# Loading q of the first token pairs in rows of 16 tokens and sorting it on TensorE, in a fused retention and bilinear feed-forward kernel

## The chip, the cores and the metric

The kernel runs on one core of one Trainium2 chip. The metric is the device time in microseconds; several runs are reported by their median. All durations below come from one profiled execution of the kernel before.

## The reference

A recurrence over time (retention with a decay per head), followed by a bilinear feed-forward layer on the 3072 = 4 x 768 tokens.

```python
# q, k, v: (4 batches, 8 heads, 768 tokens, 64), float32
gamma = 1.0 - 2.0 ** (-5.0 - np.arange(H))
for t in range(S):
    state = gamma * state + einsum('bhd,bhe->bhde', k[:, :, t], v[:, :, t])
    y[:, :, t] = 1 / sqrt(D) * einsum('bhd,bhde->bhe', q[:, :, t], state)
x = y.transpose(0, 2, 1, 3).reshape(3072, 512)
out = (x @ w_a) * (x @ w_b) @ w_out        # w_a, w_b: 512 x 1536, w_out: 1536 x 512
```

## The kernel before

**Attention.** The tokens are cut into 24 slots of 128. A decay per head becomes two tables: k is scaled by exp(-position x log gamma), q by exp(+position x log gamma) / 8, so that within a batch the retention is a masked product of q and k plus a running state. For each slot: the scaled copies `kqb` and `vb` (bf16) are made, k and q are turned so that the head dimension lies on the partitions (`kqT`), the scores `at` are formed on TensorE and masked by VectorE into `aT`, the state `st` is summed in PSUM and copied by ScalarE or VectorE (`gbd`, `gst`), and `y` is the sum of a part from the state (`inter`) and a part from the slot itself (`intra`). It is copied to `xt`, which has the feature on the partitions and is what the feed-forward layer reads.

**Pairs.** Slots 0 to 5 are handled two at a time as pairs 0, 1 and 2. `load_pair` (L93) puts two neighbouring tokens on one partition, so that one contiguous piece in memory has 2 x 64 x 4 = 512 bytes. k and q are turned on TensorE by products with the identity (`flip2`, L341; `tp`, L348), and copied from PSUM by ScalarE and VectorE (L179). `scores2`, `update2`, `inter2`, `intra2` and `leave2` (L351 to L415) are the pairs' versions of the steps. Slots 6 to 9 are turned on TensorE too (`flip`, L231), slots 10 to 23 by transposing transfers (`casts`, L225).

**Feed-forward.** Token tiles of 4, 2, 4, 4, 4, 4 and 2 slots. For tile J and each of 12 blocks `ft` of 128 features, `ffn_a` (L429) makes a = x w_a in PSUM, ScalarE copies it (`asb`, L432), `ffn_g` (L439) makes g = x w_b, and VectorE multiplies the two into `ht` (L441). `ffn_out` (L455) multiplies with w_out, ScalarE copies the result (`osb`, L177) and issues the store from its own queue (L461). Three PSUM buffers, tag `ff`, are shared in turn by a, g, o, the turned tiles and some of the scores.

**Order.** Nothing is left to a scheduler: `seq` chains every instruction of an engine to the one before in the order in which the Python runs, and the last part of the kernel writes that order out by hand. All loads stand in the SyncE queue, in the order of `LOADS`:

```python
LOADS = "p0 p1 w0 w1 w2 w3 w4 p2 w5 o0 o1 o2 o3 o4 o5 s6 s7 s8 s9 s10 s11".split()
```

(p: k, q, v of a pair; w: a sixth of w_a and of w_b; o: a sixth of w_out; s: k, q, v of a slot.) From slot 10 on, the transposing transfer of slot t and then the loads of slot t + 2 are issued from the same queue. The framework gives every transfer one of eight completion semaphores in turn, and a transfer's issue waits until the previous one on the same semaphore has landed. GpSimd (POOL) makes most of the scaled copies and casts all weights to bf16.

The tables are made at the beginning for the pairs (`tables`, L134) and during the third feed-forward block for the other slots (`late_tables`, L165).

Of the kernel before, what the change touches and what calls it, by code (L numbers as in the profile page):

```python
# [24 lines left out]
def kernel(  # L25
# [25 lines left out]
    MID = S // 2  # L51

# [40 lines left out]
    def load_pair(u):  # L93
        for nm, src in (("k", k), ("q", q), ("v", v)):
            f = raw.tile([P, H, 2, D], F32, tag=nm + "f", name=nm + "f")
            s = src[0, :, 2 * u * P : 2 * (u + 1) * P, :].rearrange("h (p two) d -> p h two d", two=2)
            seq(nc.sync.dma_start(out=f, in_=s))
            for par in range(2):
                raws[nm, 2 * u + par] = f[:, :, par, :]
# [24 lines left out]
    issue_loads(6)  # L124
    lgr = const.tile([P, 1, H], F32, name="lgr")
# [8 lines left out]
    def tables(pattern, channel):  # L134
        posp = const.tile([P, NCH, 1], F32, name=f"posp{channel}")
        seq(nc.gpsimd.iota(posp, pattern=pattern, base=-MID, channel_multiplier=channel,
                           allow_small_or_imprecise_dtypes=True))
        earg = const.tile([P, NCH, H], F32, name=f"earg{channel}")
        seq(nc.vector.tensor_tensor(earg, posp.to_broadcast([P, NCH, H]),
                                    lgr.to_broadcast([P, NCH, H]), op=ALU.mult))  # L140
        ktab = const.tile([P, NCH, H, 1], F32, name=f"ktab{channel}")
        qtab = const.tile([P, NCH, H, 1], F32, name=f"qtab{channel}")
        seq(nc.scalar.activation(ktab[:, :, :, 0], earg, AF.Exp, scale=-1.0))
        seq(nc.scalar.activation(qtab[:, :, :, 0], earg, AF.Exp, bias=bq))
        tabs.append((ktab, qtab))

    tables([[2 * P, PAIRS], [1, 2], [0, 1]], 2)
    make_identity(nc, ident)
# [4 lines left out]
    for par in range(2):  # L153
        m = const.tile([P, 1, P], BF16, name=f"mask{par}")
        seq(nc.gpsimd.memset(m, 1.0))
        for c in range(2):
            mc = m[64 * c : 64 * c + 64]
            seq(nc.gpsimd.affine_select(out=mc, in_=mc, compare_op=ALU.is_ge, fill=0.0,
                                        base=-par, pattern=[[0, 1], [1, 2], [2, 64]],
                                        channel_multiplier=-2))  # L160
        masks.append(m)
# [8 lines left out]

    wa_bf = wpool.tile([P, KT, DFF], BF16, name="wa_bf")
# [28 lines left out]
    def scaled(eng, t, i):  # L200
        ktab, qtab = tabs[0] if t < 2 * PAIRS else tabs[1]
        dst, src, tab = kqb[t][:, i], raws["kq"[i], t], (ktab, qtab)[i][:, t % NCH]
        if t < 2 * PAIRS:
            dst, src = (x.rearrange("p (hp r) d -> p hp r d", r=2) if x is src else x
                        for x in (dst, src))
            tab = tab.rearrange("p (hp r) o -> p hp r o", r=2).to_broadcast([P, HP, 2, D])
        else:
            dst = dst.rearrange("p hp r d -> p r hp d")
            src = src.rearrange("p (r hp) d -> p r hp d", r=2)
            tab = tab.rearrange("p (r hp) o -> p r hp o", r=2).to_broadcast([P, 2, HP, D])  # L210
        seq(eng.tensor_tensor(dst, src, tab, op=ALU.mult))  # L211
# [119 lines left out]
    kqT2 = {}  # L331

    def casts2(u, on):
        for t in (2 * u, 2 * u + 1):
            new_nat(t)
        for (i, par), eng in on.items():
            scaled(eng, 2 * u + par, i)
        for t in (2 * u, 2 * u + 1):
            cast(nc.gpsimd, vb[t], raws["v", t])

    def flip2(u, i, on):  # L341
        if i == 0:
            kqT2[u] = tra.tile([P, 2, 2, HP, P], BF16, tag="kqT2", name="kqT2", bufs=2)
        for pars, eng in on:
            tp = psff.tile([P, 2, HP, P], BF16, tag="ff", name="tp")[:, : len(pars)]
            for n, par in enumerate(pars):
                for hp in range(HP):
                    seq(nc.tensor.transpose(tp[:, n, hp, :], kqb[2 * u + par][:, i, hp, :, :], ident))  # L348
            cast(eng, kqT2[u][:, pars[0] : pars[0] + len(pars), i], tp)

    def scores2(u, par, ff=False):  # L351
# [6 lines left out]
        for hp in range(HP):  # L358
            for c in range(2):
                for r in range(2):  # L360
                    seq(nc.tensor.matmul(at[r][half(c), hp, :],  # L361
                                         kqT2[u][half(r), par, 0, hp, half(c)],
                                         kqT2[u][half(r), :, 1, hp, half(c)],
# [6 lines left out]
    def update2(u, c):  # L370
# [5 lines left out]
        for par in range(2):  # L376
            for hp in range(HP):
                for r in range(2):
                    t = 2 * u + par
                    seq(nc.tensor.matmul(st[half(r), hp, :], kb[t][half(c), hp, r, :],  # L380
                                         vb[t][half(c), 2 * hp + r, :],
# [5 lines left out]
    def inter2(u):  # L387
        for c in range(2):
            if (u, c) == (0, 0):
                continue  # L390
            for hp in range(HP):
                seq(nc.tensor.matmul(ys[u][c][:, hp, :], gbd[c][:, hp, :],
                                     kqT2[u][:, :, 1, hp, half(c)], start=False, stop=False,
                                     skip_group_check=True))

    def intra2(u, par, begin):
# [3 lines left out]
        for hp in range(HP):  # L400
            for r in range(2):
                for c in range(2):
                    seq(nc.tensor.matmul(ys[u][c][half(r), hp, :], vb[t][half(c), 2 * hp + r, :],  # L403
                                         aT[t][half(c), r, hp, :],
                                         start=(begin and hp == 0), stop=not begin,
                                         skip_group_check=True))

    def leave2(u):
        J, i = where[2 * u]
        if i == 0:  # L410
            xt[J] = xtp.tile([P, KT, 4 * P], BF16, tag="xt", name="xt")
        for c, eng in enumerate((nc.scalar, nc.vector)):
            cast(eng,
                 xt[J][:, :, (i + c) * P : (i + c + 1) * P].rearrange(
                     "p k (n two) -> p k two n", two=2),  # L415
                 ys[u][c].rearrange("p k (two n) -> p k two n", two=2))
# [5 lines left out]
    def ffn_a(J, ft, c0=0, c1=None):  # L422
# [5 lines left out]
        for kt in range(KT):  # L428
            seq(nc.tensor.matmul(a, wa_bf[:, kt, fs], xt[J][:, kt, c0:c1],  # L429
# [4 lines left out]
    def ffn_g(J, ft, c0=0, c1=None):  # L434
# [3 lines left out]
        for kt in range(KT):  # L438
            seq(nc.tensor.matmul(g, wb_bf[:, kt, fs], xt[J][:, kt, c0:c1],  # L439
# [7 lines left out]
    def ffn_out(J, i):  # L447
# [4 lines left out]
        for c0, c1 in cols:  # L452
# [5 lines left out]
            if c0 == DM // 2:  # L458
                continue
            b0 = DM // 2 if c0 else 0  # L460
            seq((nc.sync if c0 else nc.scalar).dma_start(out=out[n0 : n0 + P, b0:c1],  # L461
                                                         in_=osb[:, b0:c1]))
# [15 lines left out]
    K, Q = 0, 1  # L478
    casts2(0, {(K, 1): D_, (K, 0): D_, (Q, 1): D_, (Q, 0): D_})
    flip2(0, K, [((0, 1), A_)])  # L480
    flip2(0, Q, [((1,), D_), ((0,), D_)])
# [3 lines left out]
    casts2(1, {(K, 0): G_, (K, 1): G_, (Q, 0): G_, (Q, 1): D_})  # L485
    intra2(0, 1, True)
    inter2(0)
    intra2(0, 0, False)
    leave2(0)
    flip2(1, K, [((0, 1), A_)])  # L490
    update2(0, 1)
    flip2(1, Q, [((1,), D_), ((0,), D_)])
    scores2(1, 0)
    scores2(1, 1, True)
# [3 lines left out]
    intra2(1, 0, True)  # L498
    inter2(1)
    ffn_a(0, 0, 0, W2)  # L500
    ffn_a(0, 1, 0, W2)
    intra2(1, 1, False)
    leave2(1)
# [8 lines left out]
    for ft in range(2, NFT):  # L512
        if ft == 3:
            late_tables()
        if ft % FPW == 0 and ft // FPW + 1 < NW - 1:
            cast_w(ft // FPW + 1)
        if ft == 8:
            casts2(2, {(K, 0): G_, (Q, 0): G_})
            cast_w(NW - 1)
        if ft < 10:  # L520
            ffn_ab(0, ft)
        if ft == 8:
            scaled(D_, 5, K)
            scaled(D_, 5, Q)
    flip2(2, K, [((0, 1), A_)])
    flip2(2, Q, [((0, 1), D_)])
    scores2(2, 0)
    update2(2, 0)
    ffn_a(0, 10)
    scores2(2, 1)  # L530
    ffn_a(0, 11)
    intra2(2, 0, True)
    inter2(2)
    ffn_g(0, 10)
    intra2(2, 1, False)
    leave2(2)
# [49 lines left out]
```

## Time and profile before

| what | value |
|---|---|
| median of 3 runs (lowest, highest) | 240.75 us (237.88, 241.6) |
| the profiled execution: time, span | 237.4 us, 235.7 us |
| TensorE busy | 219.6 us, 93% of the span |
| VectorE, ScalarE, GpSimd busy | 96.1, 83.2, 78.6 us |
| TensorE's first instruction | 6.5 us after the span's start |
| first product of feed-forward tile 0, 1, 2 | 18.97, 47.01, 78.83 us |
| HBM read, written | 28.31 MB, 6.29 MB |
| sixth store of the output: copied, issued | 79.62, 81.19 us |

How to read it: the span is the time from the first to the last instruction of the profiled execution; the time of that execution is 1.7 us longer. Busy times say how long an engine worked, not whether anyone waited for it. In lines of the timeline the first number is the start, the second the length, both in us; then engine, line of the kernel, operation, output and inputs, shapes, count; in brackets the idle time before and what ended it. A queue that issues transfers is written SPq or ACTq. In lines of the waits, "A <- B: 7.2, 3, 6.5" says that A waited for B 7.2 us in total, 3 times, at longest 6.5 us. In the chain, each line is a start, a length and the work that stands on the chain.

### The profile page before, as it was taken

To read this page: it belongs to the slowest core of one execution; us is meant where nothing else is said; L and a number is where in the kernel's file an instruction comes from. 1 tells how busy PE (TensorE), PEld (TensorE's weight loads), DVE (VectorE), ACT (ScalarE), POOL (GpSimd) and SP (SyncE) were. 2 spreads that over 40 slices of the span, in tenths; PEclk is the share of its full clock that TensorE was granted. 3 is DMA by queue.
4 is the path that set the end of the run, shared out by engine and by line. 5 is a ranking of instruction groups with operands and counts; after the bars stand their busy time and mean duration, and the time that the engine had idled before them with its cause. 6 is when DMAs were issued, how large, how long until landed. Compare 5 with 4: busy or idle time off the path is not lost.

```text
span 235.7 us, 4955 instructions
## 1 busy us (share of the span) xinstructions
PE 219.6 (93%) x2021; PEld 121.6 (52%) x2044; DVE 96.1 (41%) x170; ACT 83.2 (35%) x162; POOL 78.6 (33%) x99
## 2 busy tenths in 40 slices
PE   0788997999999899999999999999999999999995
PEld 0566444488555344545454544454544444445874
DVE  3766347655254055634045640155630124310530
ACT  2243523443114423524234521344512242312422
POOL 3385766787763454445335530000000000000000
PEclk9999999999999999999999999999999999999999
DMA  6999999999999999999999982200002200012102
GB/s 179 290 333 352 335 273 376 342 198 219 234 260 211 245 252 172 243 181 257 210 255 172 230 93 89 89 4 0 3 0 89 89 3 0 0 47 89 45 3 89
DMA packets 91894, 38.59 MB, mean 164 GB/s; under 512 B 71776, under 2 KB 87392, under 8 KB 91872
## 3 DMA queue, kind: packets, MB, share of 16 engines
q1 hardware_dynamic: 88416, 32.12, 64.4%
q10 hardware_dynamic: 3456, 6.16, 7.3%
q8 instruction: 16, 0.26, 0.5%
q14 instruction: 6, 0.05, 0.1%
HBM read 28.31 MB, written 6.29 MB: 147 GB/s over the span
## 4 chain that ended last, share of the span: by engine, by line
PE 77%; DMA 11%; DVE 5%; issue 2%; SPq 2%; POOL 1%; ACT 1%; ACTq 0%; DVEq 0%; POOLq 0%
PE g L439 24%; PE a L429 24%; PE o L455 20%; DMA kf<-in_k_dram 6%; DMA qf<-in_q_dram 5%; PE at L254 2%; PE y L299 1%; DVE aT L367 1%; POOL kqb L211 1%; SPq L91 1%; PE tp L348 1%; PE st L270 1%; PE y L403 1%; DVE ht L441 1%; DVE kqT L179 1%
## 5 line engine op out<-in xcount | busy, mean ns | idle before, releaser
L441 DVE TENSOR_TENSOR ht<-g,asb 128x512 bf16<-128x512 f32 (+1 forms) x86 | 52.0, 604 | 109.8 <-PE g L439 88.7
L439 PE MATMUL g<-xt,wb_bf 128*128 128x512 bf16 (+1 forms) x340 | 76.0, 344 | 1.7 <-ACT asb L432 0.8
L429 PE MATMUL a<-xt,wa_bf 128*128 128x512 bf16 (+1 forms) x334 | 75.3, 344 | 0.8 <-DVE xt L179 0.2
L432 ACT CAST asb<-a 128x512 bf16<-128x512 f32 (+1 forms) x86 | 44.2, 517 | 69.4 <-PE a L429 63.6
L455 PE MATMUL o<-wo_bf,ht 128*128 128x512 bf16 (+2 forms) x303 | 63.7, 362 | 0.5
L439 PEld LDWEIGHTS <-wb_bf 128*128 128x128 bf16 x344 | 33.4, 98 | 30.3 <-issue 1.3
L429 PEld LDWEIGHTS <-wa_bf 128*128 128x128 bf16 x344 | 32.7, 98 | 27.9 <-DVE xt L179 0.7
L455 PEld LDWEIGHTS <-ht 128*128 128x128 bf16 x312 | 29.2, 98 | 31.5
L177 ACT COPY osb<-o 128x512 f32<-128x512 f32 (+2 forms) x25 | 14.1, 565 | 53.2 <-PE o L455 41.2
L211 POOL TENSOR_TENSOR kqb<-kf,ktab 128x512 bf16<-128x512 f32 x21 | 21.9, 1044 | 26.6 <-DMA kf<-in_k_dram 26.6
L211 POOL TENSOR_TENSOR kqb<-qf,qtab 128x512 bf16<-128x512 f32 x20 | 21.4, 1068 | 3.1 <-DMA qf<-in_q_dram 2.4
L259 DVE TENSOR_TENSOR aT<-at,mask 128x512 bf16<-128x512 f32 x36 | 22.3, 680 | 0.0
L179 POOL CAST vb<-vf 128x512 bf16<-128x512 f32 x24 | 14.5, 612 | 20.6 <-DMA vf<-in_v_dram 10.6
L348 PE MATMUL tp<-ident,kqb 128*128 128x128 bf16 x48 | 5.5, 280 | 7.2 <-DVE kqb L211 7.2
L308 ACT CAST xt<-y 128x512 bf16<-128x512 f32 x18 | 9.7, 589 | 3.2 <-PE y L299 3.2
L367 DVE TENSOR_TENSOR aT<-at,mask 128x512 bf16<-128x512 f32 x12 | 7.5, 684 | 2.4 <-PE at L361 2.4
L348 PEld LDWEIGHTS <-kqb 128*128 128x128 bf16 x48 | 4.0, 125 | 8.3 <-DVE kqb L211 7.8
L179 POOL CAST wa_bf<-wsta 128x1024 bf16<-128x1024 f32 x6 | 6.3, 1044 | 4.0 <-DMA wsta<-in_moe_w_a_dram 4.0
L179 POOL CAST wb_bf<-wstb 128x1024 bf16<-128x1024 f32 x6 | 6.3, 1043 | 2.7 <-DMA wstb<-in_moe_w_b_dram 2.7
L179 POOL CAST wo_bf<-wsto 128x1024 bf16<-128x1024 f32 x6 | 6.3, 1042 | 1.9 <-DMA wsto<-in_moe_w_out_dram 1.9
L177 ACT CAST gst<-st 128x256 bf16<-128x256 f32 x12 | 4.5, 373 | 6.7 <-PE st L270 6.7
L254 PE MATMUL at<-kqT 64*64 64x128 bf16 x288 | 5.8, 219 | 0.0
(47 smaller groups left out, 81.9 us busy)
## 6 DMA issues: line engine op xcount, KB each, us to landing
out_dram<-osb ACTq DMA_DIRECT2D x23, 256.0 KB, 2.1
kf<-in_k_dram SPq DMA_DIRECT2D x18, 256.0 KB, 4.6
qf<-in_q_dram SPq DMA_DIRECT2D x18, 256.0 KB, 5.1
vf<-in_v_dram SPq DMA_DIRECT2D x18, 256.0 KB, 5.4
wsta<-in_moe_w_a_dram SPq DMA_DIRECT2D x6, 512.0 KB, 8.8
wstb<-in_moe_w_b_dram SPq DMA_DIRECT2D x6, 512.0 KB, 9.0
wsto<-in_moe_w_out_dram SPq DMA_DIRECT2D x6, 512.0 KB, 8.9
kf<-in_k_dram SPq DMA_DIRECT2D x3, 512.0 KB, 7.1
```

Source lines behind the costliest of these rows:

```text
L177: seq(nc.scalar.copy(dst, src))
L179: seq(engine.tensor_copy(dst, src))
L211: seq(eng.tensor_tensor(dst, src, tab, op=ALU.mult))
L254: seq(nc.tensor.matmul(at[r][half(c), hp, :], kqT[t][half(r), 0, hp, half(c)], kqT[t][half(r), 1, hp, :], start=True, stop=True, skip_grou ...
L259: seq(nc.vector.tensor_tensor(aT[t][:, r], at[r], mask.to_broadcast([P, HP, P]), op=ALU.mult))
L348: seq(nc.tensor.transpose(tp[:, n, hp, :], kqb[2 * u + par][:, i, hp, :, :], ident))
L367: seq(nc.vector.tensor_tensor(aT[t][:, r], at[r], masks[par].to_broadcast([P, HP, P]), op=ALU.mult))
L429: seq(nc.tensor.matmul(a, wa_bf[:, kt, fs], xt[J][:, kt, c0:c1], start=(kt == 0), stop=(kt == KT - 1)))
L432: seq(nc.scalar.copy(asb, a))
L439: seq(nc.tensor.matmul(g, wb_bf[:, kt, fs], xt[J][:, kt, c0:c1], start=(kt == 0), stop=(kt == KT - 1)))
L441: seq(nc.vector.tensor_tensor(ht[J][:, ft, c0:c1], g, asbs.pop((J, ft, c0)), op=ALU.mult))
L455: seq(nc.tensor.matmul(o, ht[J][:, ft, i * P : (i + 1) * P], wo_bf[:, ft, c0:c1], start=(ft == 0), stop=(ft == NFT - 1)))
```

## The change

- q of pairs 0, 1 and 2 is loaded with one partition for each block of 16 tokens and head: a contiguous piece has 16 x 64 x 4 = 4096 bytes. It is scaled by a table `lanes` with a value for each partition and token of the block, and turned by products with columns of the identity (`pick`, a 0/1 matrix), 16 products of 64 x 64 outputs for each half, from which float32 results are copied to `qT2`. Tokens of a pair then stand in the order (token mod 16, block); the stores of the first six slots put the rows back in their places.
- `scores2`, `inter2` and `intra2` read `qT2` in steps and use the head order of the other slots. `inter2` has twice as many products with 64 columns of weights instead of 128.
- The table of the other slots is made at the beginning.
- `xt` of tiles 0 and 1 is laid out by slots, [slot, feature block, token] instead of [feature block, token].
- `warm(n)` issues n products of a zero matrix with 512 zero columns, whose result nobody reads: 28 in all.
- The order in the pairs' steps is changed: the state's second update earlier in pair 0, feed-forward products between the steps of pairs 1 and 2, pair 2 one block earlier, copies on other engines.

```diff
 def load_pair(u):
     for nm, src in (("k", k), ("q", q), ("v", v)):
+        if nm == "q":
+            f = raws[nm, "pair", u] = raw.tile([P, NJ, D], F32, tag="qf", name="qf")      # NJ = 16
+            s = q[0, :, 2 * u * P : 2 * (u + 1) * P, :].rearrange("h (b j) d -> b h (j d)", j=NJ)
+            seq(nc.sync.dma_start(out=f.rearrange("p j d -> p (j d)"), in_=s))
+            continue
...
+    def lane_table():      # called after tables(...) of the pairs; late_tables() follows the masks
+        row = const.tile([P, PAIRS, NJ], F32, name="row")
+        seq(nc.gpsimd.iota(row, ...))
+        start = const.tile([P, NJ, 1], F32, name="start")
+        seq(nc.gpsimd.iota(start, ...))
+        make_identity(nc, ident)
+        lane = ident.rearrange("p (b h) -> p b h", h=H)
+        own = const.tile([P, 2, 1], F32, name="own")
+        for i, val in enumerate((start, lgr)):
+            one = const.tile([P, NJ, H], F32, name=f"one{i}")
+            seq(nc.vector.tensor_tensor(one, lane, val.to_broadcast([P, NJ, H]), op=ALU.mult))
+            seq(nc.vector.tensor_reduce(out=own[:, i], in_=one.rearrange("p b h -> p (b h)"), ...))
+        seq(nc.vector.tensor_scalar(row, row, own[:, 0], own[:, 1], op0=ALU.add, op1=ALU.mult))
+        tab = const.tile([P, PAIRS, NJ, 1], F32, name="lanes")
+        seq(nc.scalar.activation(tab[:, :, :, 0], row, AF.Exp, bias=bq))
+        for r in range(2):
+            seq(nc.vector.tensor_copy(pick[:, r],
+                                      lane[:, :, HP * r : HP * r + HP].rearrange("p b h -> p h b")))
...
 def flip2(u, i, on):       # i == 1: q
+                tq = psff.tile([P, NJ // 2, HP, NJ], F32, tag="ff", name="tq")
+                j0 = NJ // 2 * pars[0]
+                for j in range(NJ // 2):
+                    for r in range(2):
+                        seq(nc.tensor.matmul(tq[half(r), j], ql[u][:, j0 + j, :], pick[:, r], ...))
+                cast(eng, qT2[u][:, j0 : j0 + NJ // 2], tq)
...
 def inter2(u):
-            for hp in range(HP):
-                seq(nc.tensor.matmul(ys[u][c][:, hp, :], gbd[c][:, hp, :],
-                                     kqT2[u][:, :, 1, hp, half(c)], ...))
+            for r in range(2):
+                for hp in range(HP):
+                    seq(nc.tensor.matmul(ys[u][c][half(hp % 2), 2 * r + hp // 2, :],
+                                         gbd[c][:, hp, half(r)],
+                                         qT2[u][:, :, hp, 8 * c : 8 * c + 8], ...))
...
-def leave2(u):
+def leave2(u, on):
-        xt[J] = xtp.tile([P, KT, 4 * P], BF16, tag="xt", name="xt")
+        xt[J] = xtp.tile([P, 4, KT, P], BF16, tag="xt", name="xt")
...
+    def warm(n, pool, tag):
+        idle = pool.tile([P, HP, P], F32, tag=tag, name="idle")
+        for _ in range(n):
+            seq(nc.tensor.matmul(idle, zero[:, 0, :], zero, start=True, stop=True, ...))
...
 def ffn_out(J, i):
+            if J < 2:
+                dst = dst.rearrange("(b j) d -> j b d", j=NJ)
...
+    warm(11, psat, "y1")
     casts2(0, {(K, 1): D_, (K, 0): D_, (Q, 1): D_, (Q, 0): D_})
     flip2(0, K, [((0, 1), A_)])
-    flip2(0, Q, [((1,), D_), ((0,), D_)])
+    warm(3, psat, "y1")
+    flip2(0, Q, [((1,), D_)])
+    warm(1, psat, "y1")
+    flip2(0, Q, [((0,), A_)])
+    warm(3, psat, "y1")
     scores2(0, 1)
     scores2(0, 0, True)
     update2(0, 0)
-    casts2(1, {(K, 0): G_, (K, 1): G_, (Q, 0): G_, (Q, 1): D_})
+    warm(4, psat, "y1")
+    casts2(1, {(K, 0): G_, (K, 1): G_, (Q, 1): D_, (Q, 0): D_})
     intra2(0, 1, True)
     inter2(0)
+    update2(0, 1)
+    warm(2, psff, "ff")
     intra2(0, 0, False)
-    leave2(0)
+    leave2(0, (A_, A_))
+    warm(2, psff, "ff")
     flip2(1, K, [((0, 1), A_)])
-    update2(0, 1)
     flip2(1, Q, [((1,), D_), ((0,), D_)])
-    scores2(1, 0)
-    scores2(1, 1, True)
+    warm(2, psff, "ff")
+    scores2(1, 0, True)
+    scores2(1, 1)
     update2(1, 0)
     cast_w(0)
     intra2(1, 0, True)
+    ffn_a(0, 0, 0, W2)
     inter2(1)
-    ffn_a(0, 0, 0, W2)
+    intra2(1, 1, False)
     ffn_a(0, 1, 0, W2)
-    intra2(1, 1, False)
-    leave2(1)
+    leave2(1, (A_, D_))
...
-        if ft == 8:
-            casts2(2, {(K, 0): G_, (Q, 0): G_})
+        if ft == 7:
+            casts2(2, {(K, 0): G_, (K, 1): G_})
             cast_w(NW - 1)
-        if ft < 10:
+        if ft < 9:
             ffn_ab(0, ft)
-        if ft == 8:
-            scaled(D_, 5, K)
+        if ft == 7:
+            scaled(D_, 4, Q)
             scaled(D_, 5, Q)
     flip2(2, K, [((0, 1), A_)])
-    flip2(2, Q, [((0, 1), D_)])
-    scores2(2, 0)
+    ffn_a(0, 9)
+    flip2(2, Q, [((0,), D_), ((1,), A_)])
+    ffn_g(0, 9)
+    scores2(2, 0, True)
+    scores2(2, 1)
     update2(2, 0)
     ffn_a(0, 10)
-    scores2(2, 1)
-    ffn_a(0, 11)
     intra2(2, 0, True)
     inter2(2)
+    ffn_a(0, 11)
+    intra2(2, 1, False)
+    leave2(2, (A_, D_))
     ffn_g(0, 10)
-    intra2(2, 1, False)
-    leave2(2)
     ffn_g(0, 11)
```

## The prediction

> **What bounds the kernel now.** I read the page's first two parts, then the waits of TensorE, then the timeline of the first 25 us, of 36 to 48 us and of 76 to 84 us, and last the chain.
>
> ```profile
> PE 219.6 (93%) x2021; PEld 121.6 (52%) x2044; DVE 96.1 (41%) x170; ACT 83.2 (35%) x162; POOL 78.6 (33%) x99
> ...
> PE   0788997999999899999999999999999999999995
> ...
> PEclk9999999999999999999999999999999999999999
> DMA  6999999999999999999999982200002200012102
> ```
>
> TensorE is busy for 219.6 of 235.7 us, so at most 16 us can be taken from its idle time. The row of tenths says where that lies: before its first instruction, in the slices up to 22 us, around 37 to 48 us, and (an 8) around 80 us. The DMA row says that the transfers fill the engines for the first 23 slices (135 us): whatever waits for a late transfer moves only if the whole stream moves.
>
> ```profile
> PE tp L348 <- DVE kqb L211: 7.2, 3, 6.5
> PE at L361 <- DVE kqT L179: 1.8, 3, 0.8
> PE y L403 <- DVE aT L367: 1.0, 3, 0.4
> PE g L439 <- ACT asb L432: 0.8, 2, 0.6
> PE g L439 <- DVE xt L179: 0.7, 1, 0.7
> ```
>
> All but one of TensorE's waits are in the three pairs. The fourth row is 0.6 us at 82.2 us, and it decides my forecast (the chain of 78 to 84 us, start, us, what):
>
> ```profile
> 74.98 6.14 DMA qf<-in_q_dram
> ...
> 81.19 0.34 ACTq L461
> ...
> 81.57 0.59 ACT asb L432
> ...
> 82.21 1.02 PE g L439 x4
> ```
>
> ACT has copied the sixth output tile at 79.62 us, but its store starts only at 81.19: in the built program a transfer waits for the one that last used the same of eight completion semaphores, here slot 13's q, which lands at 74.98 + 6.14 = 81.12. Behind the store stands the cast that frees a PSUM buffer, and behind that TensorE's second g of tile 2. TensorE would have been ready at 81.59 and starts at 82.21. From there to the end it is nearly gapless. So there are two clocks: TensorE's own (first 80 us) and the DMA stream's, and at 82 us the later one counts.
>
> **The change on the DMA clock.** Three q loads of 512 KB go from pieces of 512 B to pieces of 4 KB. In the trace k, q and v of pair 0 land at 5.0, 6.8 and 8.6 us, those of pair 1 at 10.45, 12.3 and 14.1: 1.8 us each; q of pair 2 takes 1.6 (32.4 to 34.0). Weight loads of the same size take 1.5 with pieces of 1 KB (15.55, 17.05), and 1.37 with 2 KB (the six wo casts, 40.54 to 47.37, each waiting for its load). 4 KB has no row. Bounds: no gain at all, or the trend carried on to 1.25, which saves 0.55 + 0.55 + 0.35 = 1.45. I take the nearest row, 1.35: 0.45 + 0.45 + 0.25, about 1.2 us earlier for everything loaded behind.
>
> Against this stands a part that nobody would see in the diff. The new order hands out the eight semaphores differently: in the listing of the changed program the sixth store waits for slot 13's **v**, not its q. v is issued at 77.03 and takes 5.2: it lands at 82.23, 1.1 us after q. So the store starts at 82.23 - 1.2 + 0.07 = 81.1 rather than 81.19, and with the same 1.02 us from there to g, TensorE goes on at about 82.1 rather than 82.21. The third and fourth stores now wait for slot 11's v (69.95 - 1.2) and slot 12's k (72.97 - 1.2), so ACT stands for 1 to 2 us each time; behind them are a gst and the xt of slots 6 and 7, which TensorE needs at 75.3, when they are done at about 73.4.
>
> **The change on TensorE's clock, first pairs.** Setup: the lane table adds to DVE one memset, two products, two reductions, a two-scalar operation, two copies and the late earg, and to POOL two iotas beside the moved mask (3 operations). The nearest rows are 0.2 us (earg 0.21, mask memset 0.21, select 0.3). DVE comes to about 4.6 us, POOL, which earg waits for, to 4.2; DVE's first kqb waits for k until 5.15. Cover of 0.5 us, cost nothing; if POOL is 1 us later than I count, 0.5 us. ACT has nothing before 7 us.
>
> q's DVE products start at 6.45 instead of 6.95 (k's products end there). The warm-up products (28 in all, 128x512) occupy TensorE where it stood. Do they help? The granted-clock row is 9 throughout, but equal work is slower early:
>
> ```profile
> 6.50 1.04 PE L348 MATMUL tp<-ident,kqb 128*128 128x128 bf16 x8 [6.50 <-DVE kqb L211]
> ...
> 9.42 1.07 PE L361 MATMUL at<-kqT 64*64 64x128 bf16 x32 [0.51 <-DVE kqT L179]
> ...
> 16.37 0.64 PE L361 MATMUL at<-kqT 64*64 64x128 bf16 x32 [0.51 <-DVE kqT L179]
> ...
> 38.03 0.83 PE L348 MATMUL tp<-ident,kqb 128*128 128x128 bf16 x12
> ```
>
> 130 ns a transpose against 69. A warm-up costs 0.215 us at the fast rate (four FFN products take 0.86), some 0.41 at the slow one, so eleven of them last to 5.0 or 5.7 us, before k is ready. I take the fast rate from 6.5 on; bounds: all fast, or all slow as far as 16 us. The Trainium skill (TensorE: Matmul & The Clock Gate, Part 1) says the clock opens after about 3.4 us of sustained activity; by it the transposes would be fast at 6.5, by the row alone not before about 10 us of sparse work.
>
> The sorting products have 64 columns of weights. The row of that shape is line 270's:
>
> ```profile
> 64.57 0.32 PE L270 MATMUL st<-vb,kqb 128*64 128x64 bf16 x8
> ```
>
> 40 ns each, 0.64 us for a half of 16, where four transposes took 0.28. (The skill's same page, under Fast Weight Load, says that only weights of 128 columns load fast; it would make a 64-column load 53 ns and a half 0.85 us. The row decides.) The PSUM result is f32, so its copy takes ACT's 0.59 or DVE's 0.7 instead of 0.42.
>
> Chain: transposes 6.5 to 7.05; three warm-ups to 7.7; half 1 to 8.35; one warm-up; half 0 to 9.2; ACT's copy 9.3 to 9.9; scores at 9.95 instead of 9.42, 16 of them in 0.42 instead of 0.67; DVE's first aT at 10.45 instead of 10.18: **0.27 later**. The four masked copies take 2.6 us as before. The second half's intra, the xt copies (now both on ACT, 0.6 each, to 15.1) and the k copy behind them (to 16.15, was 15.37) follow, then 32 sorting products (1.28, hidden under that) and DVE's two copies of 0.7 to 16.9; scores at 16.95 instead of 16.37: 0.6 later. Then it gains: the FFN products stand between the steps, and xt by slots lets g read slots 0 and 1 while 2 and 3 are written, where it now waits 0.65 for xt (fifth row of the waits). I reach the first product on slots 2 and 3 at 22.25, now 22.0: **0.25 later**. Bounds: 1.0 earlier (sorting at 27 ns, as the 64x64 products at 40.78, and copies not queued), 3.9 later (slow clock, below).
>
> **Pair 2.** From 37 to 48 us TensorE is idle for 11.0 - 9.14 = 1.86 us: waits for the products, the q copy, the masked copy, xt. The new order puts a, g between those steps; with the same durations I find each input ready (kT at 38.2, q copies at 39.3 and 39.75, masked copies at 42.0 and 43.3, xt at 45.3) and about 0.15 us of idle left. Gain 1.7, less 0.73 for sorting (32 x 40 ns for 8 x 69), the inter products being equal (16 x 39 ns for 0.62): **1.0 earlier** (bounds 0 and 1.7). The w5 casts land at 37.3 and 38.7, needed at 41.3 and 44.5: no wait.
>
> **Sum.** TensorE's clock: +0.25 - 1.0 = -0.75, so it is ready for the g of 82 us at 80.85. The DMA clock lets it start at 82.1. The later counts: the end moves by 82.1 - 82.21, **-0.1 us**; 1.25 us of what was gained goes into a longer wait. The remaining 153.5 us keep their order. Profiled execution: 237.4 - 0.1 = 237.3 us (span 235.6; 1.7 lie around it). The three runs shown, 237.88, 240.75 and 241.6, lie 0.5, 3.4 and 4.2 above the profiled one; I add 1.9, the mean of the first two: **239.2 us**. A measurement of this kernel can tell about 2% from no change, 4.8 us; nothing above comes near.
>
> **Rivals.**
> - *The gate doesn't hold* (0.20): other landings, or a stream further ahead, and TensorE keeps its gain. For: the stream's issues vary (one k issue takes 2.69 us at 49.92, its neighbours 0.9). Against: it needs 2 us more than larger pieces give. With the early bounds, 2.0 us: 235.4 profiled, 237.3 timed.
> - *Larger pieces aren't faster* (0.14): the change then doesn't do what it says, v lands at 82.23, g starts at 83.3: 1.1 later, 238.5 profiled, 240.4 timed. For: 2 KB gains only 0.13 on 1 KB.
> - *Slower: the warm-ups don't open the clock and stand in the way* (0.14). At 1.9 times the price: transposes to 7.55, three warm-ups 8.8, half 1 10.0, one 10.4, half 0 11.6, copy 12.3, scores 2.9 late; ten more warm-ups, half of them uncovered, 1.0 more: +3.9, less 1.0 of pair 2, TensorE ready at 84.5: +2.3, 239.7 profiled, 241.6 timed. It decides once TensorE is over 0.5 us late at 82. Against: the early work is sparse, and turned fast all the same by 16 us.
>
> **How the numbers follow.** The forecast has 0.52. The range runs from the gate's rival with the smallest offset (235.4 + 0.5 = 235.9) to the other two with theirs (241.9). Faster by over 2% (under 235.9) needs that rival and a low draw, or a luckier start: 0.12. Slower by over 2% (over 245.6) only the slow clock with more: 0.04. The rest, 0.84, is within.
>
> **What would show it.** Right: the transposes at 6.5 us take 0.55; q of pair 0 lands near 6.4; scores start near 10; idle in pair 2 under 0.5 us; ACT's sixth store waits for vf, and TensorE waits there for asb over 1 us. Wrong: no wait at 80 to 83 us and TensorE 1 us or more ahead there, or transposes at 130 ns.

## The result and the profile after: 1.6% slower

The changed kernel takes 242.85 us (median of 20 runs, 241.05 to 244.79), the kernel before, measured with it, 240.13 (236.96 to 241.62). The ratio is 1.0159, 95% interval 1.0124 to 1.0193; like every ratio below it is formed from the fast executions alone, those within 1.5% of the kernel's fastest, which leaves out eight of the twenty of the kernel before (the two medians over all runs stand at 1.011). The forecast of 239.2 us and its range up to 241.9 missed it. The profiled execution takes 241.28 us, its span is 239.2.

The page, first two parts:

```profile
PE 228.4 (95%) x2142; PEld 123.9 (52%) x2164; DVE 98.4 (41%) x177; ACT 84.3 (35%) x165; POOL 78.1 (33%) x100
...
PE   7787999899999989999999999999999999999995
...
PEclk9997999999999999999999999999999999999999
DMA  6999999999999999999999991300002200012102
```

TensorE is "busier" by 8.8 us, which is no gain: it counts the products of zeros and products at half speed. The 7 in the clock's row is new: one stretch at half rate, 20.77 to 24.18 us in the trace's clock records. These records also tell when TensorE's clock "opens", that is, when full speed is first granted: at 10.53 us here, at 15.75 in the kernel before. Until then equal work takes about twice as long. The transfers now fill the engines for one slice more.

TensorE's waits, longest first (waiter, line, what it waits for: us in total, times, longest):

```profile
PE tq L392 <- DVE ht L496: 1.3, 1, 1.3
PE idle L470 <- DVE zero L132: 1.3, 1, 1.3
PE tp L385 <- DVE kqb L245: 1.2, 1, 1.2
PE g L494 <- ACT asb L487: 0.9, 2, 0.7
```

The wait for the first transposes has shrunk from 6.5 to 1.2 us, because products of zeros run before it, but the transposes start at 7.36 us instead of 6.50. The fourth row is the wait at 82 us on which the forecast rested. The start, from the timeline (start, length, what; in brackets the idle time before and what ended it):

```profile
6.01 1.29 DVE L245 TENSOR_TENSOR kqb<-kf,ktab 128x512 bf16<-128x512 f32 x2 [1.04 <-DMA kf<-in_k_dram]
...
7.36 1.04 PE L385 MATMUL tp<-ident,kqb 128*128 128x128 bf16 x8 [1.24 <-DVE kqb L245]
...
8.39 1.29 DVE L238 TENSOR_TENSOR ql<-qf,lanes 128x512 bf16<-128x512 f32 x2 [1.09 <-DMA qf<-in_q_dram]
...
11.78 0.64 PE L406 MATMUL at<-qT,kT 64*64 64x128 bf16 x32
...
16.62 0.69 PE L392 MATMUL tq<-pick,ql 128*64 128x64 bf16 x32
```

In the kernel before k and q stood here:

```profile
5.15 1.29 DVE L211 TENSOR_TENSOR kqb<-kf,ktab 128x512 bf16<-128x512 f32 x2 [3.15 <-DMA kf<-in_k_dram]
6.95 1.29 DVE L211 TENSOR_TENSOR kqb<-qf,qtab 128x512 bf16<-128x512 f32 x2 [0.51 <-DMA qf<-in_q_dram]
```

k of the first pair can be used at 6.01 us (5.15 before), q at 8.39 (6.95 before; forecast 6.45), the scores start at 11.78 (9.42 before). The loads got **slower**, though not all of this is q's: in a second profile of the changed kernel (g3, below) k can be used at 5.42 and q at 7.75 us. In the trace's packet records a piece of 4 KB takes 284 ns, where one of 512 B takes 32 to 33: eight times the bytes in 8.7 times the time. And the chain around 82 us (start, length, what):

```profile
78.31 5.99 DMA vf<-in_v_dram
...
84.38 0.59 ACTq L519
...
85.00 0.59 ACT asb L487
...
85.64 1.02 PE g L494 x4
```

The mechanism is the one foreseen: the sixth store waits for slot 13's v, behind it stands the cast `asb`, behind that TensorE's second g of tile 2. But the store starts at 84.38 instead of 81.19, and that g at 85.64 instead of 82.21 (forecast 82.1). Below, the store that waits for a load, with the cast and the product behind it, is called the gate.

**One number sorts all runs**: the start of this g. From it to the end of the span it is 153.5 us in the kernel before, in the changed one and in most of the others (153.9 in the second run of the fastest); 155.0 to 155.4 where TensorE's clock drops to half for 3.41 us right after the wait (half of 3.41 is 1.7). All starts are in us, from one profiled execution each, the ratios from all executions, in the order of the sections below.

| kernel | first product on slots 2, 3 | first a of tile 1 | first a of tile 2 | second g of tile 2 | waited before it | rest of the span | ratio to before |
|---|---|---|---|---|---|---|---|
| before | 22.00 | 47.01 | 78.83 | 82.21 | 0.62 | 153.5 | 1 |
| before, second profile | 24.60 | 50.58 | 82.40 | 84.99 | 0 | 153.5 | 1.001 |
| changed | 25.60 | 50.20 | 82.15 | 85.64 | 0.74 | 153.5 | 1.0159 |
| changed, second profile | 24.25 | 48.03 | 80.75 | 86.03 | 2.53 | 153.5 | 1.0127 |
| changed, q in 512 B pieces | 21.50 | 46.29 | 78.97 | 84.42 | 2.70 | 155.2 | 1.0041 |
| changed, q from one block | 21.51 | 46.04 | 77.99 | 82.84 | 2.10 | 153.5 | 0.9892 |
| changed, stores later | 23.78 | 47.21 | 79.16 | 81.75 | 0 | 153.5 | 0.9997 |
| q as before, new order | 20.79 | 46.09 | 76.15 | 81.99 | 3.08 | 155.0 | 1.0024 |
| the same, stores later | 20.79 | 46.10 | 76.17 | 78.76 | 0 | 153.9 | 0.9778 |

### The profile page after: what moved, and what is told of

It reads as the page before. It is cut to its first block, busy times and chain, and to the rows that moved or that the text cites. A ratio compares the mean times of both kernels' runs of the same rounds, so it can differ in the third digit from the quotient of the medians.

```text
span 239.2 us, 5210 instructions
## 1 busy us (share of the span) xinstructions
PE 228.4 (95%) x2142; PEld 123.9 (52%) x2164; DVE 98.4 (41%) x177; ACT 84.3 (35%) x165; POOL 78.1 (33%) x100
## 4 chain that ended last, share of the span: by engine, by line
PE 87%; DMA 5%; DVE 3%; issue 2%; ACT 1%; SPq 1%; POOL 0%; ACTq 0%; DVEq 0%
PE a L484 25%; PE g L494 25%; PE o L510 24%; DMA vf<-in_v_dram 3%; PE at L288 2%; DMA kf<-in_k_dram 2%; PE idle L470 2%; PE y L333 1%; PE st L304 1%; PE y L450 1%; DVE ql L238 1%; PE tq L392 1%; PE y L438 1%; PE at L406 1%; PE y L324 1%
## 5 line engine op out<-in xcount | busy, mean ns | idle before, releaser
L484 PE MATMUL a<-xt,wa_bf 128*128 128x512 bf16 (+1 forms) x337 | 76.4, 346 | 0.5
L245 POOL TENSOR_TENSOR kqb<-kf,ktab 128x512 bf16<-128x512 f32 x22 | 22.9, 1044 | 26.7 <-DMA kf<-in_k_dram 16.5
L245 POOL TENSOR_TENSOR kqb<-qf,qtab 128x512 bf16<-128x512 f32 x18 | 18.8, 1043 | 2.5 <-DMA qf<-in_q_dram 2.2
L470 PE MATMUL idle<-zero 128*128 128x512 bf16 x25 | 10.2, 527 | 2.0 <-DVE zero L132 1.3
L430 ACT CAST gbd<-st 64x256 bf16<-64x256 f32 x10 | 3.7, 367 | 6.6 <-PE st L425 6.5
```

Of the source, the lines that this page charges most:

```text
L470: seq(nc.tensor.matmul(idle, zero[:, 0, :], zero, start=True, stop=True, skip_group_check=True))
L484: seq(nc.tensor.matmul(a, wa_bf[:, kt, fs], xcols(J, kt, c0, c1), start=(kt == 0), stop=(kt == KT - 1)))
```

## Experiments

### Is it q's pieces, and what about them?

**e1: the changed kernel, q in pieces of 512 B.** The values land on other partitions than the sorting wants, so the output is another one.

```diff
-s = q[0, :, ...].rearrange("h (b j) d -> b h (j d)", j=NJ)
+s = q[0, :, ...].rearrange("h (p two) d -> p h two d", two=2)
... (the tile is addressed in the same order)
```

> The changed kernel, with q of the pairs loaded again in pieces of 512 B into the new tile (its rows then lie on other partitions, so the q values used are others). Theory A (the pieces of 4 KB are slow and hold up everything behind them): k of pair 0 lands near 5.0 us instead of 5.9, its q near 6.8 instead of 8.3, the first masked copy starts near 10.4 instead of 12.25, slot 13's v lands near 82.2 instead of 84.3, and the time is 0.6% over the kernel before, where the changed kernel is 1.6% over. Theory B (warm-ups that do not open the clock, and the clock's drop at 20.8 us): the loads move, but the first product on slots 2 and 3 stays within 1 us of 25.6 and the time stays at least 1.2% over.

Measured: 241.01 us, ratio 1.0041 (0.9998 to 1.0085). q is ready at 7.22 us instead of 8.39 (7.75 in g3), and TensorE starts on slots 2 and 3 at 21.50. But at 82 us it waits 2.70 us for `asb`, and after that the clock drops:

```profile
83.20 0.55 ACTq L519 DMA_DIRECT2D out_dram<-osb  x1
...
84.42 1.07 PE L494 MATMUL g<-xt,wb_bf 128*128 128x512 bf16 x4 [2.70 <-ACT asb L487]
```

So q's pieces cost 0.8% (by the medians, 242.85 against 241.01) to 1.2% (by the ratios), and a gain made before 55 us does not reach the end.

**e2: the kernel before with q in pieces of 4 KB** (values misplaced again).

```diff
+if nm == "q":
+    s = q[0, :, ...].rearrange("h (b j) d -> b h (j d)", j=16)
+    seq(nc.sync.dma_start(out=f.rearrange("p h two d -> p (h two d)"), in_=s))
+else: ... (as before)
```

> The kernel before, with q of the pairs loaded in pieces of 4 KB as in the change (the rows lie on other partitions, so the q values used are others). Theory A: k of pair 0 near 5.9 us, its q near 8.3, slot 13's q 2 us later than 81.1, TensorE's second product of tile 2 near 84.2, time 0.9% over the kernel before. Theory B: the start moves by at most 1.5 us, is taken up by later waits, and the time is less than 0.4% over.

Measured: 241.98 us, ratio 1.0077 (1.0034 to 1.012); a piece takes 287 ns, the sixth store waits until 83.93. The load alone makes the kernel before slower.

**e3: q in two loads with pieces of 2 KB.** The layout in the chip is that of the changed kernel.

```diff
+s = q[0, :, ...].rearrange("h (b g j) d -> g b h (j d)", g=2, j=8)
+for g in (1, 0):
+    seq(nc.sync.dma_start(out=f[:, 8 * g : 8 * g + 8]..., in_=s[g]))
```

> The changed kernel, with q of each pair loaded in two transfers of 128 pieces of 2 KB (tokens 8 to 15 of the blocks first); nothing is left out. If a piece over 2 KB is what is slow: 2 KB pieces take about 88 ns as those of the output weights do, q of pair 0 lands near 6.4 us and the time is at the kernel before (0.0% to 0.3%). If it is the order of addresses (16 engines in one stretch of 64 KB of one head at a time): 2 KB pieces take about 140 ns, and the time is 1.3% to 1.6% over as with 4 KB.

Measured: 242.77 us, ratio 1.0124 (1.0056 to 1.0193). A piece of q of 2 KB takes 134 ns, one of w_out of the same size 88 ns. The same size, another price: the size is not the cause.

**e4: pieces of 4 KB from one contiguous block of 512 KB** (other tokens than the reference's).

```diff
+s = q[0].rearrange("h s d -> (h s) d")[16 * P * u : 16 * P * (u + 1), :]
+s = s.rearrange("(p j) d -> p (j d)", j=NJ)
```

> The changed kernel, with q of each pair read in pieces of 4 KB from one contiguous stretch of 512 KB (other tokens than the pair's, so the q values used are others): same size of piece and same tile, only the addresses differ. If the addresses are what is slow: pieces take about 160 ns, q of pair 0 lands near 6.4 us and the time is within 0.3% of the kernel before. If the size of the piece is: about 286 ns as in the changed kernel, and 1.3% to 1.6% over.

Measured: 164 ns a piece, 236.59 us, ratio 0.9892 (0.9823 to 0.9961). The piece came out as expected, and it is what the forecast had hoped 4 KB would give; the time is 1.1% under the kernel before, where at most 0.3% was expected. (The profiled execution is the longest of four, 238.48 us; the others take 236.4 to 236.6.) q in its timeline, against 8.39 above:

```profile
6.71 1.29 DVE L239 TENSOR_TENSOR ql<-qf,lanes 128x512 bf16<-128x512 f32 x2
```

**g1: the same block in the changed kernel's order**, sixteen pieces side by side, then 64 KB on (other tokens too); the cut shows what differs from e4.

```diff
-s = s.rearrange("(p j) d -> p (j d)", j=NJ)
+s = s.rearrange("(h b j) d -> b h (j d)", h=H, j=NJ)
```

> The changed kernel, q of a pair read from one contiguous block of 512 KB (other tokens than the reference's), but in the order of the changed kernel: sixteen neighbouring pieces of 4 KB side by side, and 64 KB on to the next sixteen, instead of 192 KB on. Theory A (the order: pieces side by side in one stretch of 64 KB hinder each other): 284 ns a piece, q of pair 0 ready near 8.4 us, ratio about 1.016. Theory B (the distance of 192 KB between heads): 160 to 170 ns, q ready near 6.7 us, ratio about 0.989, as with the contiguous block read in 32 KB stretches.

Measured: 288 ns a piece, 242.13 us, ratio 1.0106 (1.0015 to 1.0196, two executions); q is ready at 7.6 us. Same bytes, same sizes, same partitions as in e4; only which address goes to which partition differs. Theory A holds for the piece: between e4 and g1 the order does it, and 192 KB between heads are not needed for it.

**f7: rows ordered head first**, partition 16 h + b; identity columns and table follow suit.

```diff
-s = ...rearrange("h (b j) d -> b h (j d)", j=NJ)
+s = ...rearrange("h (b j) d -> h b (j d)", j=NJ)
... (identity columns and table)
```

> The changed kernel with q's 128 rows ordered head first: partition 16 h + b holds block b of head h, so that neighbouring partitions read neighbouring 4 KB pieces. Theory (the order of the addresses makes q late): a piece takes 160 to 170 ns instead of 284, k of pair 0 lands near 5.4 us and q near 6.7, the first product on slots 2 and 3 starts near 21.5; the store gate is then at 81.6 as in the run with one contiguous block of q: ratio 0.985 to 0.995. Rival (only one contiguous block of 512 KB is fast): pieces of 284 ns, 1.016 as in the changed kernel.

Measured: 248.21 us, ratio 1.0359 (1.0288 to 1.0431). Both expectations missed the time. From its timeline:

```profile
10.15 1.29 DVE L237 TENSOR_TENSOR ql<-qf,lanes 128x512 bf16<-128x512 f32 x2 [3.46 <-DMA qf<-in_q_dram]
```

q is ready at 10.15 us. The packet records show two reasons. A piece takes 306 ns, not 160 to 170, although each partition now reads on where its neighbour of the same head stops: on this point the rival was nearer. And from 4.5 to 8 us only 8 pieces of 4 KB are in flight at a time, against 16 in e4 and in the changed kernel until 5.5. The load's outermost dimension now counts 8 heads instead of 16 blocks. The Trainium skill (DMA: Bandwidth & Descriptors, Why a DMA increments its semaphore by 16 and not by 1) says that a transfer is spread over the largest number of engines, at most 16, that divides the slowest dimension of both its sides; the 8 in flight agree. Eight in flight alone would not explain it: 16 x 164 ns would be 2.6 us for the load, hardly more than the changed kernel's 8 x 284 ns = 2.3 us, and 16 x 306 ns is 4.9 us (estimates from the packet records). A part of the loss is TensorE's clock, which was at half from 9.23 to 16.06 and from 46.78 to 50.19 us. So this was no cure, and partitions that read on one after the other are not enough for a fast piece. Whether the jump of 192 KB from head to head or the eight in flight makes the pieces slow here stays open.

### The stores behind the loads

**f2: the changed kernel, third to sixth store issued later**, after `asb` of blocks 1, 3, 5 and 7 of tile 2.

```diff
+if J < 2 and n0 >= 2 * P:
+    held.append((dst, src))
+    continue
...
 seq(nc.scalar.copy(asb, a))
+if J == 2 and ft % 2 == 1 and held:
+    dst, src = held.pop(0)
+    seq(nc.scalar.dma_start(out=dst, in_=src))
```

> The changed kernel, with its third to sixth stores issued on ScalarE later (after the copies asb of tile 2's blocks 1, 3, 5 and 7), so that none stands before a cast that TensorE needs. Theory (late q holds TensorE first, the store gate adds what is left): the wait of 0.74 us for asb at 85.6 us is gone, the first products on slots 2 and 3 stay at about 25.6 us, so the kernel is 0.7 us faster than the changed one: ratio to before about 1.012 to 1.013. Rival (the stores' gate is the whole loss): with the gate gone TensorE goes on as early as its own clock allows, 3 us less, ratio 1.000. Rival (the gate does not matter): unchanged, 1.016.

Measured: 238.03 us, ratio 0.9997 (0.9958 to 1.0037). My theory expected 0.7 us and was wrong; the rival's 1.000 came out. TensorE's second g of tile 2 starts without a wait:

```profile
81.75 1.03 PE L498 MATMUL g<-xt,wb_bf 128*128 128x512 bf16 x4
```

The profile of the changed kernel had misled me: with its late clock, its half-rate stretch at 21 us and a wait of 1.26 us in pair 2 TensorE came late by itself, and little wait was left. The wait can be much longer, as the next run shows. That the ratio is just 1 is a coincidence, though: with q as before (f6, below) the same kernel is 2% faster, so late q still costs what the order gains.

**g3: the changed kernel again**, no edit.

> The changed kernel again, for a second profile. Theory (the gate levels it): if TensorE's clock does not drop at 21 us, as it did in the first profile, TensorE comes to 82 us some 1.8 us sooner, waits there 2 us or more for asb, and the time is 241 to 244 us all the same. Rival (the drop decides): without it the kernel takes 239.5 us.

Measured: 241.58 and 243.69 us. The timeline of the profiled one (241.58):

```profile
80.75 1.03 PE L484 MATMUL a<-xt,wa_bf 128*128 128x512 bf16 x4
...
84.81 0.55 ACTq L519 DMA_DIRECT2D out_dram<-osb  x1
...
85.40 1.07 ACT L487 CAST asb<-a 128x512 bf16<-128x512 f32 x2 [3.86 <-DMA vf<-in_v_dram]
...
86.03 1.02 PE L494 MATMUL g<-xt,wb_bf 128*128 128x512 bf16 x4 [2.53 <-ACT asb L487]
```

TensorE's clock opened at 6.42 instead of 10.53 us, and tile 2 starts 1.4 us earlier than in the first profile (80.75 against 82.15). All of it goes into the wait, 2.53 instead of 0.74, and the time is the same to 0.3 us. The drop at 21 us came again (20.07 us). One of the 20 executions of the result has a mean granted clock of 1.000, so no such drop; it took 241.27 us, which speaks for the theory and against the rival's 239.5.

**f3: the kernel before, stores later** (the edit of f2).

> The kernel before, with its third to sixth stores issued later on ScalarE. Theory (in the kernel before TensorE is barely behind the gate): the wait of 0.62 us at 82.2 us goes, nothing else: 0.6 us faster, ratio 0.997. Rival (the gate costs the kernel before as much as the changed one, since the profiled execution is one of its shortest): 3 to 4 us faster, 0.984.

Measured: 238.36 us, ratio 0.9924 (0.9881 to 0.9966): between the two. Some executions of the kernel before meet the gate, others not, as the next run suggests.

**g4: the kernel before again**, no edit.

> The kernel before again, for a second profile. Theory (its times from 236.5 to 241.6 us come from the moment at which TensorE's clock opens): a time near 240 us goes with a clock that opens at 20 us or later instead of 15.75, and with FFN products at half rate at 19 us. Rival: the clock opens at the same moment, and the time lies elsewhere, in loads that land later or at the stores.

Measured: 238.88 us (median of 8, 238.57 to 241.64), ratio 1.001 (0.996 to 1.006); 240.19 us in the profiled execution. Two places of its timeline:

```profile
16.36 1.07 PE L361 MATMUL at<-kqT 64*64 64x128 bf16 x32 [0.52 <-DVE kqT L179]
...
19.78 1.91 PE L429 MATMUL a<-xt,wa_bf 128*128 128x256 bf16 x8
```

```profile
83.22 0.34 ACTq L461 DMA_DIRECT2D out_dram<-osb  x1
83.60 0.58 ACT L432 CAST asb<-a 128x512 bf16<-128x512 f32 x1 [0.41 <-PE a L429]
84.99 1.03 PE L439 MATMUL g<-xt,wb_bf 128*128 128x512 bf16 x4
```

The same instructions took 0.64 at 16.37 us and 1.04 at 18.97 us in the first profile: there the clock opened at 15.75, here at 26.57. TensorE is 3.6 us late at tile 2, the store goes as soon as it is copied, and there is no wait. The profile that the forecast was built on was one of the shortest executions. The clock's row of the page shows 9 throughout for both; the opening shows in the trace's clock records and in the prices of equal work.

### The order and the products of zeros

**f4: the changed kernel without its products of zeros** (28 fewer products).

> The changed kernel without its 28 products of zeros. Theory: they set when TensorE's clock opens, not how long the path is: without them it opens between 15 and 22 us instead of 10.5, the transposes at 7.4 us take 130 ns as before, and the time moves by 1 us or less either way (ratio 1.012 to 1.020). Rival (they stand in the way): half of the 17 that follow k's arrival are on the path, 17 x 0.5 x 0.3 = 2.5 us faster, ratio 1.005. Rival (the early clock is worth much): half rate from 7 to 16 us costs the busy part of it, some 3 us more, ratio 1.028.

Measured: 240.95 us, ratio 1.0105 (1.0039 to 1.017); the clock opens at 24.82. Not slower, rather faster than the changed kernel, by 1.9 us of the medians where 1 us or less was expected, though the intervals overlap. In its profile TensorE waits 1.63 us for `xt`, which stands behind the fifth store, and 0.67 us for `asb`, and the second g of tile 2 starts at 86.08, about as in the changed kernel (85.64, 86.03): where the gate holds, an early clock mostly makes the wait longer.

**f5: q as before, everything else as changed.**

> The changed kernel's order of steps, products of zeros, early tables and xt by slots, with q's loading and turning as in the kernel before. Theory: all of the loss is q's loading; TensorE is 1.5 us ahead at 55 us, but the third to sixth stores wait behind the stream of loads and take most of that back: ratio 0.995 to 1.003. Rival (the order itself, or the products of zeros, cost something): 1.010 or more. Rival (the gate does not hold): TensorE keeps 2 us, 0.991.

Measured: 239.15 us, ratio 1.0024 (0.9984 to 1.0064), as the theory expected. The sixth store waits for slot 13's v:

```profile
80.97 0.34 ACTq L473 DMA_DIRECT2D out_dram<-osb  x1
```

TensorE reaches tile 2 at 76.15, 2.7 us earlier than in the first profile of the kernel before, waits 3.08 us, and the clock then drops from 81.65 to 85.07. The whole gain is gone.

**f6 and g2: the same with the stores later**, the fastest kernel, run twice.

> The kernel with q as before and the changed order, and the third to sixth stores issued later on ScalarE, as in the run on the changed kernel. Theory: the gate is gone and TensorE keeps what the order gained, 1.5 to 2.5 us: ratio 0.990 to 0.994, and no wait of TensorE over 0.3 us from 60 to 90 us. Rival (the gain is lost elsewhere, for instance in transposing transfers that are still late behind the loads): 0.997 or more.

> The fastest kernel so far once more (q as before, changed order, products of zeros, stores three to six later): ratio 0.980 to 0.987, and all its executions within 2 us of each other.

Measured: 234.39 us, ratio 0.983 (0.9773 to 0.9888), and 234.29 us, 0.9778 (0.973 to 0.9827): faster than the theory's 0.990, and the second a little under the 0.980 expected for it. Busy tenths and waits of the second:

```profile
PE   7989999999999999999999999999999999999994
```

```profile
PE idle L427 <- DVE zero L126: 1.3, 1, 1.3
PE y L406 <- DVE aT L370: 0.7, 2, 0.4
PE g L455 <- ACT asb L445: 0.4, 2, 0.2
```

The second g of tile 2 starts at 78.76, 3.4 us before that of the first profile of the kernel before, and no wait for `asb` is over 0.23 us. The ten executions of both runs lie within 1.6 us (233.83 to 235.4), those of the kernel before within 5.3.

**f9: the same without products of zeros.**

> The kernel with q as before, the changed order and the stores later (0.983), without its products of zeros. Theory (they open TensorE's clock some 9 us sooner, of which the products of the first pairs use about a third): 1 to 3 us slower than with them, ratio 0.988 to 0.996. Rival (they are worth nothing): 0.983. Rival (they stand in the way): 0.980 or less.

Measured: 236.84 us, ratio 0.9884 (0.982 to 0.9949), the clock opens at 23.79. Here, without the gate, the zeros are worth 0.5 to 1.1%, 1.3 to 2.5 us: the times lie apart (236.41 to 237.83 against 233.83 to 235.4), though the intervals of the ratios still overlap a little.

**f8: rows head first, stores later.**

> The same kernel, rows head first, and the third to sixth stores issued later. Theory (late q and the gate are the two causes and add up): TensorE keeps all that the order gains, 0.5 us at slots 2 and 3 and 1.4 us in pair 2, and no wait at 82 us: ratio 0.980 to 0.986, as the run with q as before and the stores later (0.983). Rival (the larger pieces are worth something by themselves): 0.975 or less. Rival (the gate is the only cause): no better than 0.995.

Measured: 243.85 us, ratio 1.017 (1.0095 to 1.0244), 1.9% under f7; the theory's 0.980 to 0.986 missed as f7's did. As there: eight pieces in flight, 317 ns a piece, q late. An order with pieces as fast as e4's that still brings the right tokens was not found.

## Why the prediction was wrong, by its own steps

- **The step that failed is q's price on the DMA clock.** 1.35 us for 512 KB was taken from a trend over sizes, with bounds of 0 and 1.45 us gained. The trend's rows (w_a, w_out) differ from q in their addresses as well as in size. A loss was excluded without a reason. With sixteen pieces in flight, a load of 128 takes 8 x 284 ns = 2.3 us (estimated from the packet records), against 1.8 before. All three q loads stand ahead of w_out in the queue, so the cast of w_out's last sixth, wherever its own load releases it, shows what they cost. It starts at 46.75 to 48.42 us in seven profiles with q in pieces of 512 B, at 49.38 to 50.20 in six with pieces of 4 KB in the change's order or g1's, 2.5 us later on average where the sum had 1.2 earlier, and at 46.05 with e4's pieces of 4 KB. Before, and after:

```profile
47.37 1.04 POOL L179 CAST wo_bf<-wsto 128x1024 bf16<-128x1024 f32 x1 [0.39 <-DMA wsto<-in_moe_w_out_dram]
...
50.12 1.04 POOL L213 CAST wo_bf<-wsto 128x1024 bf16<-128x1024 f32 x1 [0.51 <-DMA wsto<-in_moe_w_out_dram]
```

  By itself, in the kernel before (e2), the load costs 0.8%. The rival "larger pieces aren't faster" had the right subject, but ended at no gain.
- **v instead of q.** Counted as 1.1 us later; no run shows this price by itself. With q's pieces as before and the wait for v, the sixth store starts at 83.20 in e1, 2.0 later, and at 80.97 in f5, 0.2 earlier. From e1 on, q's pieces bring it to 84.38 and 84.81, 1.2 to 1.6 more, where the sum had 1.2 less.
- **From the store to g** the sum kept 1.02 us. It is 1.26: a store with rows put back in place takes 0.55 to 0.59 us to issue, not 0.34.
- **The frame was right**: two clocks, the later one counts, and the rest of the span keeps its 153.5 us. By it the changed kernel's -0.1 us becomes 85.64 - 82.21 = 3.43, and the span grew by 3.5.
- **The base was a short execution.** In one with a late clock, g starts at 84.99 without a gate; there the change costs 0.65 to 1.0 us at that point, and some 1.7 more where a further stretch at half rate comes in (four of the 20 executions have a granted clock of 0.978 or 0.979, and take 243.62 to 244.79 us). I had added 1.9 us to the profiled time as if it lay outside the span. A part of it is the clock's opening, and it moves TensorE against the gate.
- **The start.** Forecast 0.25 us later on slots 2 and 3, measured 3.6 and 2.25 in the two profiles, 0.5 *earlier* in e1: late loads, the drop of the clock at 20 to 21 us and, in the first profile, its late opening (transposes at 130 ns until 10.53). The 0.6 us lost in pair 1's scores (16.95) did not come in e1 either (16.45).
- **Sorting** was taken at 40 ns a product, the 0.32 us of the 8 in line 270's row divided by 8. Now 16 of that shape take 0.44 and 32 take 0.69 us. The three lengths lie on one line, about 0.19 us for a group and 16 ns for each product: the row was a fair one, but not to be divided by so small a count. At the full clock a pair takes 0.69 to 0.88 us instead of the sum's 1.28; in the first profile, before the clock opened, the first 16 took the 0.64 of the sum.
- **Setup** was costed at nothing, covered by the wait for k. That held: VectorE's first `kqb` is released by k's load in the timeline shown, not by the tables.
- **The rival of the zeros** (the clock stays closed, they stand in the way) holds in part for the first profile, where eleven of them in 4.87 us did not open the clock before 10.53. f4 shows no loss without them while the gate holds, f9 one without the gate.
- **Pair 2**: forecast 1.0 us earlier. From the first product on slots 2 and 3 to the first a of tile 1 the changed kernel needs 24.6 and 23.8 us, before 25.0: 0.4 and 1.2. The new order does what it should; the first profile lost 1.26 us waiting for VectorE's `ht` ahead of `tq`.
- **ACT at the third and fourth stores** was to stand for 1 to 2 us each: it stands 2.6 and 1.6 us in g3, 0.5 and 0.3 in the first profile. `xt` was not quite in time: waits of 0.2 to 1.0 us for it appear in g3, e1 and g1.
- **The rival "the gate doesn't hold"** was priced at 2.0 us "with the early bounds"; the bounds themselves, 1.0 and 1.7, with the 0.62 waited, make 3.3. With q as before and the stores out of the way (g2) that g starts 3.45 us earlier.

The ratios in a row, each step with its own run: stores later 0.9924, with the new order 0.9884, with zeros 0.9778 to 0.983, with q in blocks of 16 tokens 0.9997, with the stores back in place 1.0159. The two harmful steps cost about 2 and 1.6%; order and zeros are worth 1 to 1.5% that nobody sees while a store stands in front of a cast. The kernel before was measured anew with each group of runs, and its medians there go from 238.78 to 240.22 us, so a difference of half a per cent between ratios of two groups says little.

## What to carry to other kernels

Take a transfer's price from a row with the same address pattern, not only the same piece size, and allow for a loss when no row has it. Before counting a gain, find the next thing on the path that does not depend on it (here a store that waits for a load on the queue of an engine that TensorE needs): a gain ahead of it turns into a wait. Moving the stores out of the way was worth 0.8% alone and about 2% together with the new order and the products of zeros. Look at more than one execution: one profile may have met, or missed, a gate that the others do not.

## What the hardware showed that I had not expected

- 4 KB pieces of one 512 KB block take 164 ns when each partition reads on where its neighbour stops (e4), and 284 to 288 ns when sixteen neighbouring pieces belong to sixteen partitions 8 apart. Reading on is not enough, though: in f7 and f8 it holds within each head, with 8 pieces in flight, and a piece takes 306 and 317 ns. How memory brings this about, no run shows.
- After waits of TensorE for `asb` of 2.69 to 3.08 us (e1, e3, f5, g1) its clock fell to half for 3.41 us; after 0.74, 2.10, 2.53 and once 2.94 us (f7) it did not. The length of one wait does not settle it: in f3 the clock fell at 43.52 us after two waits of 0.8 us, in the changed kernel at 20.77 after waits of at most 0.6. Of g1:

```profile
PEclk9999999999999979999999999999999999999999
```

```profile
86.13 1.08 PE L495 MATMUL g<-xt,wb_bf 128*128 128x512 bf16 x4 [2.69 <-ACT asb L488]
...
87.01 1.91 PE L485 MATMUL a<-xt,wa_bf 128*128 128x512 bf16 x4
88.72 1.85 PE L495 MATMUL g<-xt,wb_bf 128*128 128x512 bf16 x4
```

  Four products take 1.91 us, then 1.85, instead of 1.03: the wait of 2.69 us costs some 1.7 us more (155.2 us to the end instead of 153.5). The Trainium skill (TensorE: Matmul & The Clock Gate, Part 1) says that activity is judged in windows of 3.4 us that run freely, which fits that a wait shorter than a window sometimes counts.
- With the same eleven products of zeros from 1.25 us on the clock opened anywhere between 3.95 us (e4) and 10.69 us (f2); without zeros it opened between 15.75 and 26.57 us.
